# A fused chunked scan and GELU MLP on one core: scan chunks of 128 tokens, and scan halves of 64 tokens laid out by heads

## The chip, the cores and the metric

The kernel runs on one core of a Trainium2 chip. The metric is the device time of one execution in microseconds. The kernel before takes 118.34 us, the median of three runs (118.34 to 118.67).

## The reference

A state-space scan with decay over 4 sequences of 8 heads, 768 tokens, head size 32 and state size 16, and then a two-layer MLP over the 3072 tokens of 8 x 32 = 256 features:

```python
# per batch and head, per chunk of the sequence:
cum = cumsum(log(clip(a)))                     # in the chunk
M = (C @ B.T) * exp(cum_i - cum_j) * (i >= j)  # (chunk, chunk)
y = M @ x + (C @ state) * exp(cum_i)[:, None]
state = exp(sum(log a)) * state + (B * exp(cum_end - cum_j)[:, None]).T @ x
# then, with x = y as (3072, 256):
h = x @ w_in                                   # 256 -> 2048
g = 0.5 * h * (1 + tanh(c * (h + 0.044715 * h**3)))
out = g @ w_out                                # 2048 -> 256
```

The result does not depend on the chunk's length, which the kernel is free to choose.

## The kernel before, in words

**Work.** The 3072 tokens are 24 chunks of 128 tokens (`gc`), taken in 12 pairs `u`; three pairs make one sequence `b`. In each pair the scan leaves y, transposed and in bf16, in `xm`, and the MLP runs over the pair's 256 tokens. The first layer is 8 steps `s1.u.i` of four 128x128 weight blocks against 256 tokens into one of two PSUM tiles `hp` (L710), each followed by `gelu.u.i` on ACT, which writes `gT`. The second layer is, for each of the two chunks, four steps `s2.u.k.q` of four products into `o_ps` (or `yb` for some of the last ones, L728), an eviction `oev` on ACT or DVE and a store. The kernel has 768 such matmuls in all.

**The scan.** B and C come in with the tokens of a sequence spread over partitions, are scaled with the decays (`mul`, `mulb`, `mulc`: B by the decay to the chunk's end, C by its inverse) and turned so that (head, state) lies on 128 partitions: `bh` and, with even and odd heads kept apart by a mask, `ce`. For sequences 0 and 1 TensorE turns them (`tw`, `T1`, `T` with evictions `ew`, `ce1`, `bh1`, `E`); for sequences 2 and 3 they go through DRAM and a transposing DMA (`store_s`, `turn_s`, `load_s`). `N` turns `bh` back to tokens on partitions, `bn`. Then, per pair:
- `G` (L596): the products of B and C, four row strips of 32 partitions (two heads each), one for each of the four banks of `ga` and `gb`; `M` (L606): two DVE products, one for each of the two tiles, with the triangular mask, into `m` in bf16.
- `D` (L629): the chunk's own part of the state, four column strips, into an `hp` tile; `S` (L677): the new state from the old one, on DVE; `SP` (L684): its decayed copy, block-masked by head, in bf16.
- `Y` (L651, L660): for each chunk, eight products of the state with C and eight of x with m, 128 rows deep, in four column strips of 32 outputs, into `yb`; `yev`: the copy to `xm`.
- `castx`: the pair's x from fp32 (128-token rows, loaded by `load_x`) to bf16.

Pairs 0 and 1 get x from one load in another layout: `XX` (L564) unpacks it, `XD` (L574) makes their states, `GE` and `ME` spread the first pair's mask over ACT and POOL.

**The order.** Nothing is scheduled at run time. `ORDERED` (L19) lists every step once, with the engine after a colon where there is a choice (A ACT, D DVE, P POOL, S SyncE); `~n` is n blocks of filler matmuls on zeros (L698). Each engine works through its steps in that order; waits come from the tiles that the steps share. All loads and stores but a few at the start stand in SyncE's queue.

**The start.** The decays of the first four chunks come from `aq`: `clipq`, `Rq`, `tpq`, `peq` on DVE; those of everything else from `a`: `clip` (L329), `R` (L332), `tp2` and `tp6` (L343). Then `mulb`, `mulc`, the turns, `G.0`, `XX.0`, `XD.0`, `M.0`, `Y.0`, `yev.0` lead to the first layer step `s1.0.0`, which also needs the first quarter of w_in, loaded (`load_wi`) and cast to bf16 (`wi.q.k`).

Of the kernel before, what the change touches and what calls it, by code (L numbers as in the profile page):

```python
# [8 lines left out]
FP32 = mybir.dt.float32  # L9
# [6 lines left out]
WFB = 8  # L16
# [8 lines left out]
GE.3 ME.2:P ME.3:P S.0.0 wi.0.1:P M.0.0 wi.1.1:A xn.1:A ~13 XX.1 xn.2:A wi.0.0:A XD.1 ~5 Y.0  # L25
wo.0.0:P wo.0.1:P yev.0.0.2:A G.1 S.0.1 S.1.0 pp mul1.1 S.1.1 M.1.1 M.1.0 pend:A xn.3:A load_wo.2
wi.2.0:P wi.2.1:P s1.0.0 s1.0.1 gelu.0.0 T1.1 ce1.0:D ce1.1:D s1.0.2 gelu.0.1 gelu.0.2 s1.0.3
load_wo.3 SP.3 SP.1 T1.0 s2.0.0.0.o s2.0.1.0.o SP.2 wi.3.1:P bh1:A s1.0.4 gelu.0.3 s1.0.5 G.2 tp6.0
wi.3.0:D tp6.3 gelu.0.4 gelu.0.5 wo.1.1:D Y.1 yev.1.0.2:D wo.1.0:A M.2.0 s1.0.6 s1.0.7 gelu.0.6
s2.0.0.1.o M.2.1 s2.0.1.1.o load_bc.1.0 gelu.0.7 wo.2.0:A s1.1.0 s1.1.1 gelu.1.0 wo.2.1:P  # L30
load_bc.1.1 N1 gelu.1.1 s2.0.0.2.o wo.3.1:A s1.1.2 s1.1.3 tp6.1 tp6.2 mul.1.0 s2.0.1.2.o wo.3.0:P
gelu.1.2 s2.0.0.3.o gelu.1.3 bn1:A oev.0:A recip.1.4 s1.1.4 s1.1.5 load_x.2 s2.0.1.3.o gelu.1.4
T.1.0 mul.1.1 gelu.1.5 castx.2.None:D load_x.3 s1.1.6 oev.1:A s1.1.7 E.1.0:A s2.1.0.0.o T.1.1
gelu.1.6 gelu.1.7 D.2 E.1.1:A N.1 s2.1.0.1.o s2.1.0.2.o s2.1.0.3.o S.2.0 SP.4 bn.1:D F.1
castx.3.None:A Y.2 oev.2:D D.3 G.3 yev.2.0.2:A S.3.0 load_x.4 load_bc.2.0 store.1 s2.1.1.0.o S.3.1
s1.2.0 gelu.2.0 s2.1.1.1.o s1.2.1 s2.1.1.2.o gelu.2.1 s1.2.2 s2.1.1.3.o s1.2.3 M.3.1 M.3.0
castx.4.None:D SP.6 gelu.2.2 Y.3 D.4 gelu.2.3 oev.3:A G.4 S.4.0 S.4.1 s1.2.4 mul.2.0 s2.2.0.0.o
yev.3.0.2:D gelu.2.4 s1.2.5 s1.2.6 gelu.2.5 gelu.2.6 s2.2.0.1.o s1.2.7 SP.8 s2.2.0.2.o gelu.2.7
s1.3.0 gelu.3.0 s2.2.0.3.o s1.3.1 s1.3.2 oev.4:A s2.2.1.0.o s2.2.1.1.o load_bc.2.1 load_x.6 load_x.7
M.4.1 castx.7.None:D mul.2.1 store.2 load_bc.3.1 gelu.3.1 gelu.3.2 s1.3.3 s1.3.4 s2.2.1.2.o  # L40
s2.2.1.3.o store_s.2.0 gelu.3.3 gelu.3.4 s1.3.5 load_x.5 SP.7 M.4.0 SP.9 castx.5.None:P store.3 D.5
Y.4 load_s.2 store_s.2.1 turn_s.2.0 G.5 store.0 turn_s.2.1 load_bc.3.0 oev.5:A gelu.3.5 s1.3.6
s2.3.0.0.o S.5.0 SP.10 castx.6.None:D yev.4.0.2:A gelu.3.6 s1.3.7 s2.3.0.1.o s2.3.0.2.o gelu.3.7
s1.4.0 M.5.1 s1.4.1 M.5.0 s2.3.0.3.o gelu.4.0 D.6 Y.5 store.5 oev.6:D gelu.4.1 D.7 S.6.0 S.6.1 S.7.0
S.7.1 s2.3.1.0.o store.6 load_x.8 s1.4.2 s2.3.1.1.o castx.8.None:P s1.4.3 load_x.11 load_x.9
load_x.10 store.4 yev.5.0.2:A gelu.4.2 s2.3.1.2.o F.2 s1.4.4 gelu.4.3 s2.3.1.3.o gelu.4.4 s1.4.5
mul.3.0 oev.7:A mul.3.1 G.6 s1.4.6 s2.4.0.0.o M.6.0 M.6.1 gelu.4.5 SP.12 s1.4.7 store_s.3.1
store_s.3.0 castx.10.None:P s2.4.0.1.o s2.4.0.2.o gelu.4.6 gelu.4.7 s1.5.0 s1.5.1 gelu.5.0
s2.4.0.3.o gelu.5.1 G.7 oev.8:A D.8 S.8.0 SP.16 M.7.1 Y.6 yev.6.0.2:A s1.5.2 gelu.5.2 s1.5.3
s2.4.1.0.o s2.4.1.1.o gelu.5.3 s1.5.4 turn_s.3.1 turn_s.3.0 s1.5.5 gelu.5.4 gelu.5.5 s2.4.1.2.o  # L50
s2.4.1.3.o s1.5.6 s1.5.7 SP.15 SP.13 oev.9:D gelu.5.6 s2.5.0.0.o s2.5.0.1.o gelu.5.7 s1.6.0 s1.6.1
castx.9.None:P gelu.6.0 gelu.6.1 s2.5.0.2.o s2.5.0.3.o M.7.0 load_s.3 store.7 s1.6.2 oev.10:D s1.6.3
s2.5.1.0.o s2.5.1.1.o G.8 gelu.6.2 castx.11.None:A gelu.6.3 s1.6.4 s1.6.5 s2.5.1.2.o gelu.6.4 M.8.0
s2.5.1.3.o oev.11:D M.8.1 gelu.6.5 s1.6.6 s1.6.7 gelu.6.6 s2.6.0.0.o s2.6.0.1.o D.9 SP.14 S.9.0 F.3
# [34 lines left out]
def kernel(  # L89
# [18 lines left out]
    NCH = batch * CPB  # L108
    HC = CPB // 2
    HS = S // 2  # L110
    T = 2 * Q
    d_ff = moe_w_in.shape[1]
    d_model = moe_w_in.shape[0]
    n_tokens = batch * S
# [224 lines left out]
    def f_Rq():  # L339
        scan(rq_t, acq, Q)  # L340
# [623 lines left out]
```

## Time and profile before

| | |
|---|---|
| median of three runs | 118.34 us |
| the profiled execution | 118.49 us |
| its span, first to last instruction | 116.40 us |
| TensorE clock granted in it | 1.0 |
| TensorE busy with matmuls | 109.9 us, 94% |
| DVE, ACT, POOL busy | 72.0, 73.2, 13.0 us |
| first first-layer matmul (L710) starts | 16.24 us |
| last result leaves PSUM | 113.40 us |

The span runs from the first to the last instruction; what the device time has beside it lies around the program. PE is TensorE's matmuls, PEld its weight loads, and the matmuls' ends are modelled, so for them the starts are what to read. In the slices each digit is the busy share of a fortieth of the span in tenths.

### The profile page before, as it was taken

What the parts mean: (1) busy time and instruction counts of PE and PEld (TensorE: products, weight loads), DVE (VectorE), ACT (ScalarE), POOL (GpSimd) and SP (SyncE); (2) the same over time, 40 slices, a digit from 0 to 9 for tenths busy, and PEclk for the clock granted to TensorE, in tenths of its full rate; (3) what the DMA queues carried; (4) which work ended last, traced back from release to release, by engine and by line L of the source; (5) the groups of instructions that cost most, each with busy time, mean ns of one, the idle gap of its engine ahead of it and who ended that gap; (6) DMA issues with size and microseconds to landing.
All of it is one profiled execution on the core that took longest, in us unless ns stands there. A gap on an engine that the chain in (4) does not pass through costs nothing.

```text
span 116.4 us, 3395 instructions
## 1 busy us (share of the span) xinstructions
PE 109.9 (94%) x1432; PEld 92.6 (80%) x1432; DVE 72.0 (62%) x145; ACT 73.2 (63%) x141; POOL 13.0 (11%) x30
## 2 busy tenths in 40 slices
PE   6949799999999999999999999999999999999990
PEld 2424478899888997898899988778999998999970
DVE  4996889999896994787596149978530152101110
ACT  0425967999756778668666665477477557656701
POOL 6520582400000001002040000000000000000000
PEclk9999999999999999999999999999999999999999
DMA  2999999999978699999946510210001023001212
GB/s 56 273 258 248 308 313 409 336 164 165 247 136 161 185 185 198 86 239 177 177 166 133 160 51 0 93 51 0 6 0 45 0 80 106 0 0 49 92 50 86
DMA packets 43006, 15.97 MB, mean 137 GB/s; under 512 B 36656, under 2 KB 41456, under 8 KB 42992
## 3 DMA queue, kind: packets, MB, share of 16 engines
q1 hardware_dynamic: 42800, 15.67, 55.2%
q8 instruction: 11, 0.18, 0.7%
q10 hardware_dynamic: 192, 0.10, 0.3%
q14 instruction: 3, 0.02, 0.1%
HBM read 11.04 MB, written 3.93 MB: 129 GB/s over the span
## 4 chain that ended last, share of the span: by engine, by line
PE 86%; DVE 6%; ACT 3%; issue 1%; POOL 0%; POOLq 0%; DVEq 0%
PE hp L710 37%; PE o_ps L728 33%; PE ga L596 3%; PE yb L728 3%; PE yb L660 3%; PE yb L651 2%; PE yb L698 1%; PE hp L629 1%; DVE ac L329 1%; ACT ge L611 1%; DVE r_t L332 1%; DVE ce L319 1%; DVE rt L343 1%; DVE unp L262 1%; ACT ce L315 1%
## 5 line engine op out<-in xcount | busy, mean ns | idle before, releaser
L714 ACT ACTIVATE gT<-hp 128x512 bf16<-128x512 f32 x96 | 53.6, 596 | 25.1 <-PE hp L710 24.8
L710 PE MATMUL hp<-xm,w_in_sb 128*128 128x256 bf16 x384 | 51.7, 273 | 0.1
L728 PE MATMUL o_ps<-w_out_sb,gT 128*128 128x256 bf16 x352 | 47.4, 273 | 0.0
L710 PEld LDWEIGHTS <-w_in_sb 128*128 128x128 bf16 x384 | 41.4, 114 | 2.1 <-issue 1.0
L728 PEld LDWEIGHTS <-gT 128*128 128x128 bf16 x384 | 37.1, 98 | 4.2 <-issue 0.4
L319 DVE COPY o_sb<-o_ps 128x256 f32<-128x256 f32 x12 | 5.1, 424 | 24.7 <-PE o_ps L728 22.2
L606 DVE TENSOR_TENSOR m<-ga,tri 128x1024 bf16<-128x1024 f32 x12 | 14.6, 1218 | 3.0 <-PE ga L596 2.0
L606 DVE TENSOR_TENSOR m<-gb,tri 128x1024 bf16<-128x1024 f32 x11 | 13.4, 1216 | 0.0
L698 PE MATMUL yb<-wz 128*128 128x512 bf16 (+3 forms) x32 | 8.6, 410 | 1.0 <-DVE wz L220 1.0
L684 DVE SCALAR_TENSOR_TENSOR sp_new<-s_new,pend,bmask 128x256 bf16<-128x256 f32 x17 | 8.6, 512 | 0.1
L315 ACT ACTIVATE xm<-yb 128x512 bf16<-128x512 f32 x8 | 4.8, 597 | 3.7 <-PE yb L660 2.1
L698 PEld LDWEIGHTS <-wz 128*128 128x128 bf16 x32 | 3.2, 111 | 4.6 <-issue 1.9
L677 DVE SCALAR_TENSOR_TENSOR s_new<-s_new,pend,hp 128x64 f32<-128x64 f32 x13 | 3.6, 278 | 4.9 <-PE hp L629 4.5
L317 POOL CAST x<-x_t 128x512 bf16<-128x512 f32 x4 | 2.6, 669 | 35.2 <-PE hp L710 25.2
L315 ACT ACTIVATE o_sb<-o_ps 128x256 f32<-128x256 f32 x10 | 3.8, 384 | 3.7 <-PE o_ps L728 3.7
L660 PE MATMUL yb<-m,x 128*32 128x128 bf16 x192 | 6.1, 220 | 0.0
L651 PE MATMUL yb<-ce,sp_new 128*32 128x128 bf16 x160 | 5.2, 220 | 0.0
L596 PE MATMUL ga<-ce,bh 32*128 32x256 bf16 x48 | 4.7, 272 | 0.1
L596 PE MATMUL gb<-ce,bh 32*128 32x256 bf16 x48 | 4.7, 273 | 0.0
L728 PE MATMUL yb<-w_out_sb,gT 128*128 128x256 bf16 x32 | 4.3, 273 | 0.0
L660 PEld LDWEIGHTS <-x 128*32 128x32 bf16 x192 | 3.7, 97 | 0.7 <-issue 0.7
L319 DVE CAST xm<-yb 128x512 bf16<-128x512 f32 x4 | 2.7, 683 | 1.6 <-PE yb L660 1.6
(109 smaller groups left out, 76.1 us busy)
## 6 DMA issues: line engine op xcount, KB each, us to landing
out_dram<-o_sb SPq DMA_DIRECT2D x24, 128.0 KB, 2.6
x_t<-in_x_dram SPq DMA_DIRECT2D x20, 128.0 KB, 3.2
wf<-in_moe_w_in_dram SPq DMA_DIRECT2D x4, 512.0 KB, 6.8
wf<-in_moe_w_out_dram SPq DMA_DIRECT2D x4, 512.0 KB, 8.3
bc_t<-in_B_dram SPq DMA_DIRECT2D x3, 384.0 KB, 4.8
bc_t<-in_C_dram SPq DMA_DIRECT2D x3, 384.0 KB, 6.3
scr<-bc SPq DMA_DIRECT2D x4, 192.0 KB, 3.0
x_t<-in_x_dram SPq DMA_DIRECT2D x1, 512.0 KB, 4.5
```

The lines of the kernel that those rows point to most:

```text
L315: nc.scalar.activation(o, i, AF.Copy)
L319: nc.vector.tensor_copy(out=o, in_=i)
L596: nc.tensor.matmul(out=gbank(g)[:, 256 * k:256 * k + 256], lhsT=bh_of(2 * u + k)[gs], rhs=ce_of(2 * u + k)[gs], start=True, stop=True, til ...
L606: nc.vector.tensor_tensor(out=m_of(u)[:, 2 * i:2 * i + 2].rearrange("p g k e t -> p (g k e) t"), in0=gx[i].rearrange("p g (k t) -> p (g k) ...
L651: nc.tensor.matmul(out=y4[32 * j:32 * j + 32, k, w], lhsT=sp[:, 32 * h:32 * h + 32], rhs=ce_of(gc)[:, h % 2], start=first(j), stop=False, ...
L660: nc.tensor.matmul(out=y4[32 * j:32 * j + 32, k, w], lhsT=X16[u][:, k, 32 * h:32 * h + 32], rhs=m[:, h // 2, h % 2, :], start=first(j), st ...
L677: nc.vector.scalar_tensor_tensor(out=s_new, in0=state[("s", gc - 1)], scalar=pend_of(gc), in1=d, op0=ALU.mult, op1=ALU.add)
L684: nc.vector.scalar_tensor_tensor(out=sp_new.rearrange("p (g d) -> p g d", g=4), in0=(XN[0][:, H * D:H * D + 64] if gc == 0 else state[("s" ...
L698: nc.tensor.matmul(out=t[:, 0:m * 128], lhsT=wz, rhs=w3.to_broadcast([128, m, 128]), start=True, stop=True, skip_group_check=True)
L710: nc.tensor.matmul(out=hp[:, j * T:(j + 1) * T], lhsT=w_in_k[:, w, q, k], rhs=xm[:, w, u * T:(u + 1) * T], start=(w == 0), stop=(w == 1))
L714: nc.scalar.activation(gts[u][:, 2 * i:2 * i + 2], hps.pop((u, i)).rearrange("p (j t) -> p j t", j=2), AF.Gelu_apprx_tanh)
L728: nc.tensor.matmul(out=ops[gc], lhsT=gts[u][:, fi, k * Q:(k + 1) * Q], rhs=w_out_sb[:, fi, :], start=(fi == 0 and (u > 0 or k == 0)), stop ...
```

## The change

Pairs 2 to 11 are treated as halves (`n`, 0 to 3 in a pair; `hc` over all) of 64 tokens. Tokens of a half lie on 64 partitions; the lower 64 hold heads 0 to 3 and the upper 64 heads 4 to 7.
- `G`: 16 products of 32 rows by 64 outputs over 64 tokens of the two head parities (128 columns), in `ga`'s two banks only. `MM`: one DVE product of 128x1024 in place of two.
- `D`: 16 products, 64 rows deep, into `yb`. `SS`: one state update per half. `SV`: the decayed, head-masked bf16 copies of up to two states, on POOL or DVE, in place of `SP`.
- `YY`: per half eight products of state and C and eight of x and m, all 64 rows deep with 32 outputs and 64 columns, into the two banks of `gb`; `yev` reads those.
- `castx`: two steps a pair (one for each half of the heads), each with two instructions on 64 partitions. `N`, `N1` and `load_s` lay `bn` out alike: 64x64 products with the identity in place of 128x128 transposes.
- The decay scan restarts every 64 tokens; `endq`, `gpar`, `tri2`, `pm` are new small constants or products. The buffers for fp32 weights go from 8 to 7.
- The whole of `ORDERED` is new. Its start and one later stretch are shown.

```diff
-WFB = 8
+WFB = 7
 ORDERED = """
-c_wz c_ident load_a.1:S c_m4 load_a.0:A c_zero c_unp c_sel load_aq.1:A clip R load_x4 tp2
-load_aq.2:A load_aq.0:A load_aq.3:S load_bc0.0 load_bc0.1 load_wi.1 load_bc1.0 c_warm c_tri x4.0:A
-clipq Rq load_wi.0 c_m8 c_bmask c_par tpq peq mulb:D load_bc1.1 recip0 ~78 ppq ~7 tw.0 ew.0.0:A
-ew.1.0:A recip1 c_cz pendq:D mulc.0:D ~9 tw.1 mulc.1:D ew.0.1:D ew.1.1:A tw.2 load_wo.0 ew.1.2:A
-wi.1.0:A x4.1:P ew.0.2:D load_wi.2 pe load_wi.3 load_wo.1 ~3 XX.0 xn.0:A mul1.0 G.0 XD.0 GE.2 SP.0
...
+c_wz load_aq.1:A load_bc0.0 c_ident c_bmask load_aq.3:A c_zero load_aq.0:S load_aq.2:S c_sel c_unp
+load_bc0.1 load_x4 load_a.0:A load_a.1:S c_m4 c_gpar clipq Rq c_cz c_tri load_wi.0 peq tpq c_tri2
+load_wi.1 load_wo.0 recip0 ~48 ppq mulc.1:D load_wi.2 mulb:P c_m8 load_wi.3 ~18 tw.2 tw.0 c_warm
+ew.0.2:A ew.1.2:A pendq:D mulc.0:D ew.1.0:D ew.0.0:D tw.1 ew.0.1:A load_wo.1 x4.1:A ~9 G.0 clip R
+load_bc1.0 x4.0:P XX.0 load_bc1.1 XD.0 GE.3 S.0.0 SP.0 GE.2 ew.1.1:A xn.1:A xn.0:A ME.3:P ME.2:P ~21
+XX.1 XD.1 M.0.0 wi.0.1:A wi.1.0:D Y.0 S.0.1 xn.2:A pe S.1.0 yev.0.0.2:A wi.0.0:P wo.0.0:P wi.1.1:P
+G.1 tp2 load_x.2 S.1.1 SP.1 M.1.0 load_wo.2 wo.0.1:P pp pend:A s1.0.0 s1.0.1 M.1.1 gelu.0.0 gelu.0.1
...
+E.1.0:A gelu.2.0 mul.1.1 gelu.2.1 T.1.1 E.1.1:A F.1 castx.3.1:D N.1 s1.2.2 s2.1.1.2.o s2.1.1.3.o
+s1.2.3 oev.3:D gelu.2.2 bn.1:A gelu.2.3 s1.2.4 D.3 SS.3.0 SS.3.1 G.3 gelu.2.4 SS.3.2 castx.4.1:D
+SS.3.3 s1.2.5 load_bc.2.1 s2.1.0.0.o MM.3 s2.1.0.1.o s1.2.6 s2.1.0.2.o s2.1.0.3.o mul.2.0 SV.3.0:P
+SV.3.1:P load_x.6 load_x.9 castx.4.0:P D.4 YY.3 castx.5.1:A oev.2:D gelu.2.6 gelu.2.5 G.4 s1.2.7
...
+YX = gx[1][:, :, 0:T].rearrange("p w (n t) -> p w n t", t=L)     # L = 64
+def halves(out, bh, n):                                           # N, N1
+    for k in range(n):
+        for w in range(2):
+            ws = slice(L * w, L * w + L)
+            nc.tensor.matmul(out=out[ws, k], lhsT=bh[ws, L * k:L * k + L], rhs=ident[ws, ws],
+                             start=True, stop=True, tile_position=(L * w, L * w), skip_group_check=True)
 def f_G(u):
+    if u > 1:
+        for k in range(2):
+            for i in range(2):
+                for g in range(4):
+                    gs = slice(32 * g, 32 * g + 32)
+                    w = g // 2
+                    nc.tensor.matmul(out=gx[0][L * w:L * w + L, g % 2, (2 * k + i) * Q:(2 * k + i) * Q + Q],
+                                     lhsT=bh_of(2 * u + k)[gs, L * i:L * i + L],
+                                     rhs=ce_of(2 * u + k)[gs, :, L * i:L * i + L], start=True, stop=True,
+                                     tile_position=(32 * g, L * w), skip_group_check=True)
+        return
...
+def f_MM(u):
+    nc.vector.tensor_tensor(
+        out=m_of(u).rearrange("p g n e t -> p (g n e) t"),
+        in0=gx[0].rearrange("p g (n t) -> p (g n) t", t=L),
+        in1=tri2.rearrange("p (n t) -> p n t", n=1).to_broadcast([128, 16, L]), op=ALU.mult)
 def f_D(u):
-    DT[u] = psh.tile([128, 512], FP32, name="hp")
+    DT[u] = yb[:, 0:T].rearrange("p (n d) -> p n d", d=L)
...
         for g in range(4):
+            ws = slice(L * (g // 2), L * (g // 2) + L)
+            nc.tensor.matmul(out=DT[u][32 * g:32 * g + 32, n],
+                             lhsT=bn_of(gc)[ws, n % 2, 32 * (g % 2):32 * (g % 2) + 32],
+                             rhs=x_of(u)[ws, n, 64 * (g % 2):64 * (g % 2) + 64],
+                             start=True, stop=True, tile_position=(ws.start, 32 * g),
+def f_YY(u):                                                      # mm: start on the first of each (w, j)
+    for n in range(4):
...
+        for part in range(2):
+            if not part and hc % HPB == 0:
+                continue
+            for j in range(4):
+                for w in range(2):
...
+                    if part:
+                        mm(w, j, n, x_of(u)[ws, n, js], MT[u][ws, j // 2, n, j % 2, :], True)
+                    else:
+                        t, c = state[("sp", hc)]
+                        mm(w, j, n, t[ws, c, js], ce[ws, j % 2, ts], False)
+def f_SV(u, q, eng):
...
+    (nc.gpsimd if eng == "POOL" else nc.vector).tensor_tensor(
+        out=t[:, f:2].rearrange("p i (g d) -> p i g d", g=2),
+        in0=sts[:, h0 - 1:h0 - 1 + n].rearrange("p i (o d) -> p i o d", o=1).to_broadcast([128, n, 2, 64]),
+        in1=pm[:, :, b, c + f:c + 2].rearrange("p g (i o) -> p i g o", o=1).to_broadcast([128, n, 2, 64]),
+        op=ALU.mult)
```

More of the change, by code (lines that the diff above doesn't have):

```diff
@@ L25 @@
[L25 to L30, printed above, removed]
@@ L269, in c_par, with c_gpar, c_tri2 @@
                                     op=ALU.add, axis=mybir.AxisListType.X)
+    def c_gpar():
+        bmp = bmask.rearrange("p (w g e d) -> p g w e d", w=2, g=2, e=2)
+        for g in range(2):
+            nc.vector.tensor_reduce(out=gpar[:, g:g + 1], in_=bmp[:, g, :, :, 0], op=ALU.add,
+                                    axis=mybir.AxisListType.XY)
+    def c_tri2():
+        for i in range(2):
+            nc.vector.tensor_copy(out=tri2[L * i:L * i + L], in_=tri[L * i:L * i + L, L * i:L * i + L])
     def c_sel():
@@ L339, in f_Rq @@
     def f_Rq():
-        scan(rq_t, acq, Q)
+        scan(rq_t, acq, endq, Q)
     def turn(o, i, n):
@@ L367, in f_R @@
     def f_R():
-        scan(r_t, ac, HS)
+        scan(r_t, ac, ends, HS)
     def f_tp2():
@@ L679, in f_S, with f_SS @@
                                            op0=ALU.mult, op1=ALU.add)
-        state[("s", gc)] = s_new
+    def f_SS(u, q):
+        hc = 4 * u + q
+        d = DT[u][:, q]
+        if hc % HPB == 0:
+            nc.vector.tensor_copy(out=sts[:, hc % (2 * HPB)], in_=d)
+        else:
+            nc.vector.scalar_tensor_tensor(out=sts[:, hc % (2 * HPB)], in0=sts[:, (hc - 1) % (2 * HPB)], scalar=pend_of(hc), in1=d,
+                                           op0=ALU.mult, op1=ALU.add)
     def f_SP(gc):
-        sp_new = st.tile([128, 256], BF16, name="sp_new")
+        sp_new = spp.tile([128, 256], BF16, name="sp_new")
@@ L689, in f_SP @@
         state[("sp", gc)] = sp_new
+    def f_SV(u, q, eng):
+        b, c = divmod(4 * u + 2 * q, HPB)
+        f = int(c == 0)
+        n = 2 - f
+        t = spp.tile([128, 256], BF16, name="sp_new").rearrange("p (i d) -> p i d", i=2)
+        h0 = (4 * u + 2 * q + f) % (2 * HPB)
+        (nc.gpsimd if eng == "POOL" else nc.vector).tensor_tensor(
[3 more added lines that the diff above has]
+            op=ALU.mult)
+        for i in range(f, 2):
+            state[("sp", 4 * u + 2 * q + i)] = (t, i)
@@ L797 @@
     pp.takes("hp", pd)
+    pm_ = add("D", f_pm, deps=[pd, cgp])
     ce, bh, bn = {}, {}, {}
```

312 lines of the change are left out of this document (178 added, 134 removed).

## The prediction

> **What bounds the kernel now.** I read the page first (busy shares, slices, the chain that ended last), then the chain of waits in order of time, then single stretches of the timeline.
>
> ```profile
> span 116.4 us, 3395 instructions
> PE 109.9 (94%) x1432; PEld 92.6 (80%) x1432; DVE 72.0 (62%) x145; ACT 73.2 (63%) x141; POOL 13.0 (11%) x30
> PE   6949799999999999999999999999999999999990
> DMA  2999999999978699999946510210001023001212
> GB/s 56 273 258 248 308 313 409 336 164 165 247 136 161 185 185 198 86 239 177 177 166 133 160 51 0 93 51 0 6 0 45 0 80 106 0 0 49 92 50 86
> PE 86%; DVE 6%; ACT 3%; issue 1%; POOL 0%; POOLq 0%; DVEq 0%
> ```
>
> TensorE owns 86% of the chain and is full from the sixth slice of 2.91 us on; DVE and ACT have a third of the span free, POOL nine tenths. Before that the transfers are full and the DVE leads the chain.
>
> ```profile
> 6.97 0.24 DVE acq L329
> 15.10 0.23 PE yb L660 x8
> 16.24 0.61 PE hp L710 x4
> 60.48 0.87 PE hp L710 x8
> 61.35 0.87 PE o_ps L728 x8
> 113.40 0.38 ACT o_sb L315
> ```
>
> So there are two parts. **The start** runs until the first first-layer matmul (L710) at 16.24. **The stream** runs from there to 113.40, 97.2 us, when ACT takes the last result. A layer matmul costs 0.87 / 8 = 0.109 us; 768 of them make 83.8. The other 13.3 us are scan products, transposes, changes of the array's shape and the few waits. What follows 113.40 stays as it is: the new order ends in the same copy and store.
>
> **The stream, part by part.** One stretch of TensorE's timeline shows a whole pair:
>
> ```profile
> 30.32 1.36 PE L728 MATMUL o_ps<-w_out_sb,gT 128*128 128x256 bf16 x11
> 31.61 0.29 PE L651 MATMUL yb<-ce,sp_new 128*32 128x128 bf16 x8
> 31.73 0.28 PE L660 MATMUL yb<-m,x 128*32 128x128 bf16 x8
> 31.85 0.28 PE L651 MATMUL yb<-ce,sp_new 128*32 128x128 bf16 x8
> 31.96 0.28 PE L660 MATMUL yb<-m,x 128*32 128x128 bf16 x8
> 32.07 0.23 PE L629 MATMUL hp<-x,bn 128*32 128x64 bf16 x8
> 32.23 0.28 PE L596 MATMUL ga<-ce,bh 32*128 32x256 bf16 x2
> 32.24 0.28 PE L596 MATMUL gb<-ce,bh 32*128 32x256 bf16 x2
> ...
> 32.56 0.61 PE L728 MATMUL o_ps<-w_out_sb,gT 128*128 128x256 bf16 x4
> ```
>
> Outputs (Y): 32 matmuls from 31.61 to 32.07, 0.46 us, 14 ns each, because four column strips of 53 ns run at once. States (D): 8 in 0.16. Gram (G): 8 in 0.33. Eleven layer matmuls would be over at 30.32 + 1.20 = 31.52, yet Y begins at 31.61: a change of shape costs about 0.1 us. Taking it out of D and G as well leaves D 0.06 and G 0.23.
>
> Y becomes YY: 64 matmuls of 64 x 32 strips and 64 columns, eight strips at once. The nearest operation is the state product of pairs 0 and 1, also 64 columns, also eight strips, alternating two banks:
>
> ```profile
> 14.40 0.18 PE L574 MATMUL hp<-x4b,bc0s 32*32 32x64 bf16 x1 [0.48 <-ACT x L315]
> ...
> 14.53 0.19 PE L574 MATMUL o_ps<-x4b,bc0s 32*32 32x64 bf16 x1
> 14.65 0.45 PE L698 MATMUL yb<-wz 128*128 128x512 bf16 x2
> ```
>
> 32 of them start in 0.13 us, 4 ns each, so 64 take 0.26; the upper bound is Y's 14 ns each, 0.90. I take 0.26, the row with the same strips: -0.20 a pair, and **-1.9** over ten, of which three have no state product in their first part. D becomes 16 matmuls of 64 columns on four strips: four rounds instead of two, +0.06, **+0.6**. G becomes 16 of 128 columns on four strips: the same columns streamed, 0. The transposes that make B by token become 64 x 64 products, 32 for 8, with half the columns and two strips at once: 0. Shape changes, counted along the order from the first L710 step to the end: 36 before, 42 after (YY and D share a shape, as Y and D did, but more blocks stand alone), **+0.6**. Sum: **-0.7**.
>
> At one place a rule speaks against this. Before, row strips that run at once write different banks: G's four strips four banks (ga and gb twice), L574's two strips hp and o_ps. In the new G, two row strips share a bank, on different partitions; in the new D, all share yb. No run so far shows that case. The Trainium skill, "TensorEngine Tiling (Array Packing)", section "Gotcha 1: PSUM Pressure", says that different row tiles cannot access the same PSUM bank simultaneously. If strips that share a bank queue, D and G take twice their streams; that is the first rival. I take the value without queueing, because these strips also differ in columns, like Y's, which share a bank.
>
> DVE: one mask product of 1.22 us a pair instead of two, no 512-ns state copies, but four state updates and some SV copies:
>
> ```profile
> L606 DVE TENSOR_TENSOR m<-ga,tri 128x1024 bf16<-128x1024 f32 x12 | 14.6, 1218 | 3.0 <-PE ga L596 2.0 <-PE gb L596 1.0
> L684 DVE SCALAR_TENSOR_TENSOR sp_new<-s_new,pend,bmask 128x256 bf16<-128x256 f32 x17 | 8.6, 512 | 0.1
> L677 DVE SCALAR_TENSOR_TENSOR s_new<-s_new,pend,hp 128x64 f32<-128x64 f32 x13 | 3.6, 278 | 4.9 <-PE hp L629 4.5
> L317 POOL CAST w_in_sb<-wf 128x512 bf16<-128x512 f32 x4 | 2.4, 616 | 1.3 <-DMA wf<-in_moe_w_in_dram 1.3
> ```
>
> About -12.2 - 8.7 + 20 x 0.28 + 5 x 0.5, some 13 us off the DVE. It is worth nothing: the stream hides it. New waits: YY behind SV, of which 15 of 20 sit on POOL. POOL's multiply is not shown; the cast reads 512 elements in 0.62, SV reads 2 x 256, so 0.3 to 1.2, I take 0.6. Behind an SV in POOL's queue stand only input casts; the worst chain, D.3 - three SS - SV - cast - D.4, comes to 0.9 + 0.6 + 0.8 = 2.3 us, beside G.3 and six layer steps of four matmuls, 2.9 us. D now waits for yb instead of hp, which frees hp for the layers. All that: 0, while that cover lasts.
>
> **The start.** Now the DVE does the 64 x 384 clip, scan and turns (3.2 us) ahead of the small ones that feed the first pair:
>
> ```profile
> 3.65 1.06 DVE L274 COPY selp<-sel 128x128 f32<-128x128 f32 x1
> 3.68 0.95 POOL L255 MEMSET cz<- 128x1024 bf16 x1
> 3.79 1.12 DVE L329 TENSOR_SCALAR ac<-a_t 64x384 f32<-64x384 f32 x1
> 4.94 0.95 DVE L332 TENSOR_TENSOR_SCAN r_t<-ac,ends 64x384 f32<-64x384 f32 x1
> 5.92 0.98 DVE L343 STREAM_TRANSPOSE rt<-r_t 32x64 f32<-32x64 f32 x4
> 6.97 0.23 DVE L329 TENSOR_SCALAR acq<-aq_t 128x128 f32<-128x128 f32 x1
> 8.17 0.68 DVE L417 TENSOR_TENSOR bc0s<-bcf,rt 128x512 bf16<-128x512 f32 x1
> 9.21 0.76 DVE L410 TENSOR_TENSOR cz<-bcf,pt 128x256 bf16<-128x256 f32 x2
> ```
>
> The new order puts clipq first and the large steps behind the first pair's evictions, where the DVE otherwise waits for XD. Its own work ahead of clipq would then end near 5.0: the constants up to 3.79, the memset that holds them until 4.63, and four added small ones (0.4). The small loads that clipq needs land then too:
>
> ```profile
> aq_t<-in_a_dram ACTq DMA_DIRECT2D x3, 16.0 KB, 4.4
> ```
>
> They are issued half a microsecond earlier, with B's 256 KB ahead of them instead of x4's 512 KB, so 4.4 us is their upper bound and 5.0 a fair landing. From clipq to the first mulc lie 2.24 us now, 0.6 of them mulb. mulb moves to POOL, 0.6 (one cast) to 1.2 us (two operands of 512; I take this), from 6.4 to 7.6. The memset row shows that the copy and the clip, short otherwise, both end only after POOL's memset at 4.63. So I let mulc wait for mulb as well and put the second mulc's end at 8.4; not waiting would be worth 0.7. The Trainium skill, "SBUF — State Buffer", section "Who interferes with whom", calls the ports that the two engines share an exclusive lock, for the copies' modes and for a two-input DVE product against a reading POOL. The trace agrees for the copy and the clip (1.06 and 1.12 us); no run so far shows the product.
>
> From the last mulc's end, 9.97, to the first L710 lie 6.3 us now. The new chain from 8.4 is two evictions on the DVE (0.9), G.0, ACT's cast of x4 until 10.0, XX and XD until 10.5, then SP 0.5, M 1.2 and their hand-overs until 12.5, Y 0.5, its eviction 0.7 and the one small product pp ahead of the layers: 5.7 us. The first L710 comes at **14.1**, **-2.1**. Bounds: 12.9 (no blocking and a short mulb) and 15.7 (the small loads as late as now).
>
> Part of it is paid back. The weight casts of now start when their loads land (DMA row: saturated until slice 11):
>
> ```profile
> 16.49 1.18 POOL L317 CAST w_in_sb<-wf 128x512 bf16<-128x512 f32 x2 [0.20 <-DMA wf<-in_moe_w_in_dram]
> 18.81 0.62 POOL L317 CAST w_in_sb<-wf 128x512 bf16<-128x512 f32 x1 [1.14 <-DMA wf<-in_moe_w_in_dram]
> 21.37 0.62 POOL L317 CAST w_out_sb<-wf 128x512 bf16<-128x512 f32 x1 [1.94 <-DMA wf<-in_moe_w_out_dram]
> ```
>
> Moving the two small B and C loads (0.26 MB) behind wo.1 brings wi.3 about 1 us forward at 0.3 MB/us, to 17.7; two POOL casts, which queue behind wi.2's, end at 18.9. The stream would want them at 18.4: **+0.5**. wo.2 comes 0.6 later (x.2 and the small loads ahead of it), 2 us before need; wo.3, on seven buffers, waits for the first casts at 12.5, and the B and C loads of sequence 1 behind it on SP are then still early. ACT, with 9 us of work beside 9.5 of TensorE where pair 1's second half meets wo.3's casts and E.1, may add **+0.3**.
>
> **Sum.** -0.7 - 2.1 + 0.8 = -2.0 against the profiled execution's 118.49 (span 116.40 and 2.09 around it): **116.5**. The median shown is 118.34, 0.1% under it.
>
> **Rivals.**
> 1. *Row strips queue at a shared bank* (slower). D +0.12 and G +0.23 a pair and B's products, twice as long, +0.4: +3.9, so 120.4. It turns the sign once more than 2.0 us are lost, half of this. For it: every row-strip product now in the kernel writes banks of its own. Against: Y's column strips share one.
> 2. *The loads set the start anyway.* If weights land no earlier than now, wi.3's casts end at 19.9, 1.0 behind the forecast, and wo.1's at 21.3, another 0.5: the payback is 2.3 instead of 0.8, and 118.0 is left. For it: DMA full in slices 2 to 11. Against: casts of now are done 1 us and more ahead of use.
> 3. *The start goes better*: no blocking, 12.9, and no payback: -0.7 - 3.3: 114.5.
> 4. *TensorE cannot be fed 64 small products at 4 ns.* The 32 at 14.40 had waited 0.48 us behind ACT, so they may have been queued. At 8 ns YY takes 0.51, +2.5: 119.0; at Y's 14 ns, 122.9.
> 5. *The order adds waits* in mid-stream (POOL slower than 1.2, a load late): +3, 119.5.
>
> **Chances.** Forecast 50%, rival 1 13%, 2 13%, 3 13%, 4 5%, 5 6%. Differences within 0.3% (0.36 us) are what a measurement of this kernel cannot tell from none. Faster: 46 of the forecast's 50, rival 3, and 5 of rival 2, 64%; same: 3 + 6, 9%; slower: 27%. The range leaves out rival 4 and the far ends of 3 and 5, and takes in rival 1: 114.2 to 120.6.
>
> **What would show it.** The first L710 at 14.1 (12.9 to 15.7) and clipq near 5.0. YY's 64 starts in 0.26 us; D's 16 in 0.12 and G's in 0.23, twice that under rival 1. TensorE's digits 9 from slice 6 on, no wait over 0.3 us after 25 us. DVE near 60 us busy. It is wrong if TensorE sits idle for SV, MM or casts past pair 3, or if the first L710 stays near 16.

## The result, and the profile after

The changed kernel takes 121.75 us, the median of four runs (120.11 to 123.43), beside 118.44 us for the kernel before on the same chip (118.34 to 118.67, four runs). The ratio is 1.0158, with an interval of 1.0132 to 1.0185: 1.6% longer, some 120.3 us by the ratio, where 116.5 us and faster had been forecast. Some executions of a kernel are up to 4 us longer than its others; the ratios leave those out, and of the profiles read below three are of such executions, those of 123.43 us (changed kernel), 120.08 us (experiment 3) and 122.88 us (`start_weights`).

The page of an execution of 119.92 us (experiment 1 below), 1.43 above the profiled execution of before. TensorE, slices, transfers, chain:

```profile
span 118.2 us, 4471 instructions
PE 112.3 (95%) x1931; PEld 95.5 (81%) x1931; DVE 65.1 (55%) x165; ACT 75.4 (64%) x146; POOL 25.7 (22%) x55
PE   6979999999999999999999999999999999999990
DMA  3999987997999767999994940021001201021102
PE 78%; DVE 7%; DMA 7%; SPq 3%; issue 2%; ACT 0%; DVEq 0%
```

TensorE is now full from the fourth slice on, and stays so to the end. The kernel is slower although its bounding engine starts earlier and hardly idles: the time is in what TensorE does. Its timeline where the layers begin (L820 is the first layer's matmul here, L710 before):

```profile
14.16 0.39 PE L416 MATMUL hp<-pe,selp 64*128 64x48 f32 x2 [0.29 <-DVE pe L410]
14.48 1.06 PE L820 MATMUL hp<-xm,w_in_sb 128*128 128x256 bf16 x8
```

The stream starts 1.76 us earlier, at 14.48 for 16.24, and all of that and as much again is lost behind it. The table adds up the time from each matmul's start to the next one's, by kind, from the first layer matmul to the last; a change of shape and a wait fall to the matmul ahead of them. The third column is an experiment, the changed kernel behind the old start, told below.

| us | before | changed | changed, old start |
|---|---|---|---|
| first layer matmul | 16.24 | 14.48 | 16.91 |
| 768 layer matmuls | 85.47 | 85.90 | 85.81 |
| outputs (Y; YY and the Y of pair 1) | 5.49 | 6.53 | 6.06 |
| states (D) | 0.95 | 2.26 | 2.27 |
| B times C (G) | 3.29 | 3.63 | 3.68 |
| turns (T, N) | 1.65 | 1.83 | 1.82 |
| filler on zeros | 0 | 0.21 | 0.21 |
| stream | 96.85 | 100.38 | 99.86 |

The outputs were to fall by 1.9 us; they rose, by 1.04, of which 0.4 is a wait in the Y of pair 1, and by 0.57 behind the old start, where that wait is missing. One step YY in TensorE's timeline (start, busy time, then the tile, the shape of the strip and the count):

```profile
26.50 0.82 PE L820 MATMUL hp<-xm,w_in_sb 128*128 128x256 bf16 x6
27.25 0.22 PE L698 MATMUL gb<-ce,sp_new 64*32 64x64 bf16 x8
27.29 0.21 PE L698 MATMUL gb<-m,x 64*32 64x64 bf16 x8
27.32 0.21 PE L698 MATMUL gb<-ce,sp_new 64*32 64x64 bf16 x8
27.35 0.21 PE L698 MATMUL gb<-m,x 64*32 64x64 bf16 x8
27.48 0.26 PE L698 MATMUL gb<-ce,sp_new 64*32 64x64 bf16 x8
27.54 0.26 PE L698 MATMUL gb<-m,x 64*32 64x64 bf16 x8
27.61 0.26 PE L698 MATMUL gb<-ce,sp_new 64*32 64x64 bf16 x8
27.68 0.26 PE L698 MATMUL gb<-m,x 64*32 64x64 bf16 x8
27.86 0.72 PE L838 MATMUL o_ps<-w_out_sb,gT 128*128 128x256 bf16 x5
```

Read the starts. The first four groups of eight come 30 to 40 ns apart, 4 ns a product, as forecast. Then there is a pause (27.35 to 27.48), and the last four come 60 to 70 ns apart, over 8 ns a product. From the first to the 64th start it is 0.49 us, and 0.61 to the next layer matmul. Nine of the ten YY steps of this execution break at the 33rd product. Three of the nine have 56 products (the first half of a sequence has no state product), and there the 33rd is another product, in the middle of the third half:

```profile
65.32 0.21 PE L698 MATMUL gb<-ce,sp_new 64*32 64x64 bf16 x8
65.45 0.26 PE L698 MATMUL gb<-m,x 64*32 64x64 bf16 x8
```

In the tenth step 16 products of D, of the same strips, are mixed in, and the row breaks behind the 32nd of both kinds together, which is YY's 16th.

### The profile page after: what moved, and what is told of

Read it like the earlier page. It is cut to its first block, busy times and chain, and to the rows that moved or that the text cites. A ratio compares the mean times of both kernels' runs of the same rounds, so it can differ in the third digit from the quotient of the medians.

```text
span 121.7 us, 4471 instructions
## 1 busy us (share of the span) xinstructions
PE 113.3 (93%) x1931; PEld 96.0 (79%) x1931; DVE 65.5 (54%) x165; ACT 75.5 (62%) x146; POOL 25.9 (21%) x55
## 4 chain that ended last, share of the span: by engine, by line
PE 64%; SPq 15%; DMA 10%; DVE 5%; issue 2%; POOL 1%; ACT 0%; POOLq 0%
PE hp L820 27%; PE o_ps L838 25%; SPq L161 5%; DMA bc_t<-in_B_dram 5%; DMA x_t<-in_x_dram 5%; PE gb L698 4%; SPq L181 3%; PE yb L838 3%; PE ga L638 3%; SPq L196 2%; SPq L200 1%; PE yb L688 1%; DVE x L342 1%; DVE m L658 1%; SPq L168 1%
## 5 line engine op out<-in xcount | busy, mean ns | idle before, releaser
L820 PE MATMUL hp<-xm,w_in_sb 128*128 128x256 bf16 x384 | 52.9, 274 | 0.2 <-POOL w_in_sb L340 0.2
L820 PEld LDWEIGHTS <-w_in_sb 128*128 128x128 bf16 x384 | 41.0, 114 | 2.4 <-POOL w_in_sb L340 0.4
L793 POOL TENSOR_TENSOR sp_new<-sts,pm 128x256 bf16<-128x256 f32 (+1 forms) x15 | 8.8, 595 | 55.2 <-DVE sts L775 48.1
L775 DVE SCALAR_TENSOR_TENSOR sts<-sts,pend,yb 128x64 f32<-128x64 f32 x33 | 9.2, 278 | 3.8 <-PE yb L688 3.2
L808 PE MATMUL yb<-wz 128*128 128x512 bf16 (+2 forms) x26 | 8.3, 475 | 1.1 <-DVE warm L231 1.1
L342 DVE CAST x<-x_t 64x256 bf16<-64x256 f32 x22 | 7.3, 334 | 1.5 <-DMA x_t<-in_x_dram 1.2
L340 POOL CAST x<-x_t 64x256 bf16<-64x256 f32 x12 | 5.2, 430 | 8.5 <-DMA x_t<-in_x_dram 8.0
L698 PE MATMUL gb<-m,x 64*32 64x64 bf16 x320 | 6.5, 194 | 0.1
L698 PE MATMUL gb<-ce,sp_new 64*32 64x64 bf16 x296 | 6.0, 195 | 0.0
L638 PE MATMUL ga<-ce,bh 32*64 32x128 bf16 x160 | 4.4, 220 | 1.7 <-DVE ce L544 1.7
L698 PEld LDWEIGHTS <-sp_new 64*32 64x32 bf16 x296 | 4.5, 89 | 1.2 <-issue 0.8
L698 PEld LDWEIGHTS <-x 64*32 64x32 bf16 x320 | 4.9, 89 | 0.6 <-issue 0.6
```

Of the source, the lines that this page charges most:

```text
L342: nc.vector.tensor_copy(out=o, in_=i)
L638: nc.tensor.matmul(out=gx[0][L * w:L * w + L, g % 2, (2 * k + i) * Q:(2 * k + i) * Q + Q], lhsT=bh_of(2 * u + k)[gs, L * i:L * i + L], rhs ...
L698: nc.tensor.matmul(out=YX[32 * j:32 * j + 32, w, n], lhsT=lhsT, rhs=rhs, start=(w, j) not in fresh, stop=stop, tile_position=(L * w, 32 * ...
L775: nc.vector.scalar_tensor_tensor(out=sts[:, hc % (2 * HPB)], in0=sts[:, (hc - 1) % (2 * HPB)], scalar=pend_of(hc), in1=d, op0=ALU.mult, op ...
L793: (nc.gpsimd if eng == "POOL" else nc.vector).tensor_tensor(out=t[:, f:2].rearrange("p i (g d) -> p i g d", g=2), in0=sts[:, h0 - 1:h0 - 1 ...
L808: nc.tensor.matmul(out=t[:, 0:m * 128], lhsT=wz, rhs=w3.to_broadcast([128, m, 128]), start=True, stop=True, skip_group_check=True)
```

## The experiments

In the rows of waits, the engine, tile and line that waited stand left of the arrow and what released them right of it; then come the us in all, the number of waits and the longest. Two theories stood against each other. **Issue**: TensorE has some 32 small products ready when it comes to them, and what lies behind is fed at over 8 ns each. **Transfers**: the loss is waits for loads that the new order makes late. For the second spoke the waits of the execution profiled first, that of 123.43 us:

```profile
PE ga L638 <- DVE ce L544: 1.7, 1, 1.7
PE yb L688 <- DVE x L342: 0.6, 1, 0.6
```

G.7 waits for sequence 2's turned C, and D.2 for pair 2's x; before has neither.

**1. The changed kernel again, with no edit.**

> The changed kernel as it is, for a profile of an undisturbed execution. Two theories stand for the loss. Issue: TensorE holds some 32 small products ready; what comes beyond them starts 8.3 ns apart instead of 4, so that an output step (YY) takes 0.5 us instead of 0.26 and the scan products and shape changes cost about 2.5 us more than before, in every execution. Transfers: the loss is waits for loads (x of pair 2, the turned C of sequence 2), 4 us in the execution profiled so far, and the products are as forecast. Issue expects 120.1 to 120.7 us with YY at 0.5 us and waits of 1 us or less in all; transfers expects waits that differ from execution to execution and still add to 2 us or more here.

120.94 us (119.92 to 123.33), ratio 1.0120 (1.0096 to 1.0144). The waits of the execution of 119.92:

```profile
PE yb L808 <- DVE warm L231: 1.1, 1, 1.1
PE hp L455 <- POOL m L259: 0.5, 1, 0.5
PE hp L416 <- DVE pe L410: 0.3, 1, 0.3
PE hp L808 <- ACT gT L824: 0.2, 1, 0.2
PE yb L736 <- DVE sp_new L780: 0.2, 1, 0.2
```

The first three lie ahead of the layers. Neither D.2 nor G.7 waits, and the kernel still takes 1.2% longer than before. Waits for loads make 2.3 us of the execution of 123.43; they do not explain this one.

**2. The changed kernel behind the old start.**

```diff
-c_wz load_aq.1:A load_bc0.0 c_ident c_bmask load_aq.3:A c_zero load_aq.0:S load_aq.2:S
+c_wz c_ident load_a.1:S c_m4 load_a.0:A c_zero c_unp c_sel load_aq.1:A clip R load_x4 tp2
...
 s1.0.0 s1.0.1
```

> The changed kernel with the old start and the new order behind it, first matmul near 16.2. Issue: the stream's loss of 2 to 3 us stands alone, 121 to 122 us. Transfers: with the loads in the old order the stream is as forecast, 118 to 119 us.

122.47 us (121.86 to 122.57), ratio 1.0317 (1.0288 to 1.0347). Its list of waits, whole:

```profile
PE yb L806 <- DVE wz L226: 1.1, 1, 1.1
PE hp L377 <- DVE peq L372: 1.0, 1, 1.0
PE hp L607 <- ACT x L336: 0.5, 1, 0.5
PE hp L806 <- ACT gT L822: 0.2, 1, 0.2
PE hp L597 <- ACT ce L336: 0.2, 1, 0.2
```

Only the 0.2 of L806, the filler, lies in the stream. So the last column of the table is a stream without transfer waits, and it is 3.0 us longer than that of before: outputs +0.57, D +1.32, G +0.39, layers +0.34, filler 0.21, turns 0.17. The new start is worth about 2 us to the changed kernel (121.86 against 119.92).

**3. Half the products in YY.** The kernel leaves out the products of state and C in pairs 2 to 11.

```diff
-                if not part and hc % HPB == 0:
+                if not part:
                     continue
```

> The changed kernel without the products of state and C in pairs 2 to 11 (the output then lacks what comes from earlier halves), so that an output step has 32 products instead of 64. Issue: 32 are held ready and start in 0.13 us, 0.38 less a pair, 3 to 3.8 us less in all: 116.8 to 117.8. Transfers: 32 products at 4 ns are 0.13 less a pair, 1.3 at most, and the waits for the turned C swallow part: 119.2 to 120.

118.88 us (117.37 to 120.67, ten runs), ratio 0.9985 (0.9951 to 1.0018). Its YY:

```profile
28.75 0.31 PE L698 MATMUL gb<-m,x 64*32 64x64 bf16 x32
28.99 0.72 PE L838 MATMUL o_ps<-w_out_sb,gT 128*128 128x256 bf16 x5
```

32 products and the change of shape take 0.24 us instead of 0.61, and L698 2.50 us in all instead of 5.54. Half the products cost two fifths of the time, and the whole disadvantage is gone with them. The time meets neither expectation: by the ratios it is 1.6 us below that of the changed kernel, where L698 saves 3.0. In the one profiled execution, of 120.08 us, G.7 waits 1.5 us and D.2 0.5 for loads; where the rest goes in the shorter ones no profile shows. So YY's products carry the loss; that does not yet say whether the second 32 are slow because they are the second 32.

**4. YY in two steps of 32**, a few layer steps apart; everything is computed.

```diff
-    def f_YY(u):
+    def f_YY(u, half):
-        for n in range(4):
+        for n in (2 * half, 2 * half + 1):
...
-YY.2 s2.0.0.3.o s2.0.1.3.o gelu.1.6
+YY.2.0 s2.0.0.3.o s2.0.1.3.o YY.2.1 gelu.1.6
```

> The changed kernel with each YY step cut in two steps of 32 products (two heads each), the second two layer steps behind the first (one layer step for pair 6); everything else as in the changed kernel. Issue (some 32 small products are held ready, what lies behind them starts 8.3 ns apart): now each half finds its 32 products ready, 0.13 us each with 0.1 us per additional change of shape, so L698 falls from 0.5 us a pair to 0.26 in starts, and the time stays or falls by about 0.5 us (10 x (0.25 - 0.2)), 119.4 to 120.1. If 8.3 ns is instead a property of the second half of the products themselves (their banks, columns or operands) and not of a stock that ran out, the second halves still start 8.3 ns apart, the changes of shape come on top, and the time is about 2 us higher, 122. Transfers: no change in the waits, 120 as before.

123.49 us (122.88 to 124.96), ratio 1.0390 (1.0355 to 1.0426). By the time alone that would be the second alternative. The timeline says otherwise (L699 is YY here, L839 the second layer):

```profile
26.92 0.22 PE L699 MATMUL gb<-ce,sp_new 64*32 64x64 bf16 x8
26.96 0.21 PE L699 MATMUL gb<-m,x 64*32 64x64 bf16 x8
26.98 0.21 PE L699 MATMUL gb<-ce,sp_new 64*32 64x64 bf16 x8
27.01 0.21 PE L699 MATMUL gb<-m,x 64*32 64x64 bf16 x8
27.16 1.05 PE L839 MATMUL o_ps<-w_out_sb,gT 128*128 128x256 bf16 x8
28.14 0.22 PE L699 MATMUL gb<-ce,sp_new 64*32 64x64 bf16 x8
28.18 0.21 PE L699 MATMUL gb<-m,x 64*32 64x64 bf16 x8
28.20 0.21 PE L699 MATMUL gb<-ce,sp_new 64*32 64x64 bf16 x8
28.23 0.21 PE L699 MATMUL gb<-m,x 64*32 64x64 bf16 x8
```

Both halves start within 0.12 us, and the second half does so in all ten pairs. The very products that came at 8.3 ns come at 4 ns when layer matmuls stand ahead of them; the second of the two theories of the pace falls. And the added time:

```profile
PE hp L821 <- ACT xm L337: 1.7, 2, 0.9
PE hp L821 <- DVE xm L341: 0.4, 1, 0.4
PE o_ps L839 <- DVE o_sb L341: 0.3, 1, 0.3
```

2.4 us of new waits: the second halves stand so late that the layers wait for the copy of y. Without them the kernel would be near the unsplit one. In the rows the split saves 0.25 us a pair of pace (0.12 twice for 0.49) and adds two changes of shape at about 0.1.

**5. Two attempts on the transfer waits.** The DMAs of sequence 2's turned C and B ahead of other loads, and pair 2's x ahead of the two small loads of pair 2's B and C (`load_bc1`; the expectations, here and below, call them sequence 1's):

```diff
-store.1 load_x.7 load_x.8 ... load_s.2 store_s.2.1 ... turn_s.2.1 ... turn_s.2.0
+store_s.2.1 load_x.7 turn_s.2.0 load_x.8 turn_s.2.1 load_s.2 ... store.1
```
```diff
-load_bc1.0 x4.0:P XX.0 load_bc1.1 ... G.1 tp2 load_x.2
+load_x.2 load_bc1.0 x4.0:P XX.0 load_bc1.1 ... G.1 tp2
```

> The changed kernel with the DMAs of sequence 2's turned C and B (the second store, the two turns) issued ahead of the x loads of pairs 7 and 8 and of store.0 on SP, where they stood behind them. Transfers: the wait of G.7 for the turned C of sequence 2 (1.9 us in the profiled run of the changed kernel) is gone in every execution, so the slowest executions come about 1.9 us down, the lower ones, which had no such wait, stay near 120.0. Issue: the same for the lower ones; L698 stays at 0.5 us a pair, and the kernel stays about 1.2% slower than the kernel before.

> The changed kernel with pair 2's x load issued ahead of the two loads of sequence 1's B and C, where it stands behind them. Transfers: D.2 never waits for x (1.3 us in the profiled run of the changed kernel), so the slowest executions lose that, and the lower ones stay near 120.0 unless B and C of sequence 1 (T1) now come late, which would cost up to 1 us. Issue: no change of the lower executions, 119.9 to 120.3; L698 stays at 0.5 us a pair.

The first took 127.53 us (126.51 to 128.03), ratio 1.0737 (1.0692 to 1.0783): a miss. Its largest wait in the profiled execution (127.85 us):

```profile
PE yb L686 <- DMA bn<-scr: 3.9, 2, 3.4
```

D.6 now waits for the untransposed B of the same sequence, which was issued behind the turns; a new wait took the place of the old. Behind its 3.4 us the granted clock is 0.58 of full speed from 55.5 to 58 us and 0.78 from 58 to 61, which by an estimate from these figures costs up to another 1.7 us. The second took 121.36 us (120.64 to 124.86), ratio 1.0233 (1.0203 to 1.0263): 1% more than the changed kernel, not less, though its profiled execution (120.64) shows no wait in the stream above 0.3. One execution of five took 124.86 us; it has no profile, so whether D.2 waited in it is not shown. What makes the loads late in some executions and not in others is left open.

**6. The new start with the old pairs.** Eight kernels, all the kernel before with another order, which begins as the changed one does. In `start_alone` the new order goes up to `s1.0.1`, in `start_alone2` up to `s1.1.3`, in `start_long` up to `s1.1.7`, and the old order follows with what is left. `new_order_old_pairs` has the new order throughout, each old step at its counterpart's place. `start_best` is `start_alone2` without the filler and with two steps moved. In `start_weights` the loads of wo.2 and wo.3 are also issued ahead of `load_bc1`'s two, and T1 and G.2 come later; in `start_weights2` `load_bc1`'s two stand between wo.2 and wo.3; in `start_weights3` mul.1.0 is also moved ahead of M.2.1, and T.1, D.3 and G.3 later. Two cuts show pair 3 in `new_order_old_pairs` beside the changed kernel (-), and `start_best` beside `start_alone2` (-):

```diff
-castx.3.0:P ... castx.3.1:D ... D.3 SS.3.0 SS.3.1 G.3 ... MM.3 ... SV.3.0:P SV.3.1:P ... YY.3
+castx.3.None:D ... D.3 S.3.0 G.3 S.3.1 ... M.3.0 M.3.1 ... SP.6 ... Y.3
```
```diff
-wo.0.0:P wi.1.1:P G.1 tp2 load_x.2 ... s1.0.2+4
+wi.1.1:P wo.0.0:P G.1 tp2 ... s1.0.2 ... s1.1.5 load_x.2
```

> The kernel before with the new order's start alone (everything up to the first first-layer matmul, its loads too), then the old order. Issue: the start is worth what the first matmul shows, it begins near 14.6 instead of 16.24, so 116.9 to 117.4 us. Transfers: the loads give it back, one of the casts of the weights or x of pair 2 comes late and 118 to 119 us remain.

> The kernel before with the changed kernel's order up to layer step s1.1.3, so that the loads and the products of sequence 1's B and C stand where the changed kernel has them, and the old order, old pairs 2 to 11, from there on. The start was worth -1.8 us at the first layer matmul and the stream cost +3.5, so this kernel should keep the first without the second. Issue: first L710 near 14.5, the stream within 1 us of before's 96.9 (the filler of four products +0.2, up to +0.8 given back in waits for weights or in sequence 1's steps), 117.0 to 117.9, faster than before. Transfers: the same start, but the loads of pairs 2 to 4 land later as they do in the changed kernel, and the stream gives back 2 us or more, so 118.5 or above.

> As the run with the new start and the old pairs, with three edits: no filler products on s1.0.2, the cast of wi.1.1 ahead of that of wo.0.0 on POOL (its wait was 0.4 us in the changed kernel), and pair 2's x load left at its old place behind the B and C loads of sequence 1. Issue: 0.2 to 0.6 us below that run, 116.6 to 117.5, a version below both kernels. Transfers: pair 2's x lands later still, and its D waits: 0.5 us or more above that run.

> The kernel before, its pairs 2 to 11 unchanged (Y of 128-row products, two mask products, state copies on the DVE), but everything in the changed kernel's order: the new start, the loads, weight casts, B and C of the sequences, layer steps and stores where the changed kernel has them, each step of an old pair at the place of its new counterpart. Issue (the halves themselves cost the stream 3 us, and the order's only cost is small): Y 5.5, D 0.95, G 3.3 as before, first layer matmul near 14.5, so about 117 us, below both kernels, if the longer mask products (2.4 for 1.2 us a pair) find cover at those places; up to 1 us more if not. Transfers (the order's loads and waits are what costs): the waits stay with the order, and it stays at 119.5 to 120.5 like the changed kernel.

> As the run before it in this call, but only up to the layers of pair 2 (all weight casts and sequence 1's products B and C in the new order, which the shorter version of this experiment cut in two), the old order from there on. Issue: the lead of 1.7 us is kept past the weights, less 0.2 for the filler, so 117.0 to 118.0. Transfers: the loads behind the start are late and the lead is lost, 118.7 or above.

> The kernel with the new start, old pairs and old order from pair 2 on (no filler), with the loads of wo.2 and wo.3 issued ahead of the two loads of sequence 1's first B and C, their casts at once behind them, and the products that need that B and C (mul1, T1, N1 and G.2) four layer steps later. In the earlier run wo.3 landed at 25.35 (22.66 in the kernel before) and the layers waited 0.7 us for its cast and some 1 us for B and C. If eight outstanding DMAs ahead of the weights are what ate the lead (loads theory): wo.3 lands near 22, no wait for w_out, first layer matmul near 14.7 and 117.2 to 118.2, below both kernels. If not (the old pairs themselves need the time between pair 1 and pair 2): 119 as the earlier run.

> As the run before it in this call, with the two loads of B and C between wo.2 and wo.3 instead of behind both. Loads theory: wo.3 lands near 23, B and C about 1 us earlier than in that run, 117.2 to 118.5. Otherwise 119 as the earlier run.

> As the last run, with sequence 1's first product (mul.1.0) between pair 2's two mask products on the DVE instead of behind them, and its turns T.1, N.1 and pair 3's D.3 and G.3 two to four layer steps later. In the last run the weights no longer waited, and what was left was one wait of 1.9 us of T.1 for that product. Loads theory: with it gone the stream is within 1 us of before's 96.9 behind a first layer matmul near 14.7, 117.2 to 118.2, below both kernels. Otherwise a new wait takes its place and it stays at 119 or above.

| kernel | median, us | ratio | interval | largest new wait of TensorE, us in all |
|---|---|---|---|---|
| start_alone | 124.54 | 1.0485 | 1.0451 to 1.0519 | T1 for a mask product queued on the DVE, among others behind two products that wait 1.2 for loads, 5.5 |
| start_alone2 | 119.80 | 1.0058 | 1.0026 to 1.0091 | second layer for w_out's cast, 1.2 |
| start_best | 119.21 | 1.0057 | 1.0032 to 1.0081 | the same, 0.7 |
| start_long | 120.89 | 1.0190 | 1.0150 to 1.0230 | Y for its state copies, 1.2 in 2 |
| new_order_old_pairs | 129.43 | 1.0901 | 1.0852 to 1.0951 | first layer for hp, 5.8 in 11 |
| start_weights | 121.59 | 1.0236 | 1.0201 to 1.0271 | T.1 for its product on the DVE, 2.1 |
| start_weights2 | 120.57 | 1.0180 | 1.0137 to 1.0223 | the same, 1.9 |
| start_weights3 | 121.51 | 1.0242 | 1.0205 to 1.0279 | D.2 for hp, 1.5 |

All take longer than before, by 0.6% to 9%, although in all of them the layers begin at 14.6 to 15.2. Expected were some 117 to 118 in most, so here Issue's expectation failed each time; its account of YY is not touched by that, for there is no YY in these kernels. Two of the rows, from the waits of the whole new order with the old pairs and of the last kernel:

```profile
PE hp L707 <- ACT gT L711: 5.8, 11, 0.7
```
```profile
PE hp L626 <- ACT gT L711: 1.5, 1, 1.5
```

In the old pairs D lies in an hp tile, so the layers have one tile left until S has read it. The new order was written for D in yb, and with D in hp it stalls eleven times. The other kernels trade one wait for the next: when the weights came early (start_weights2: no wait for a cast left), T.1 was late; when T.1 was moved, D.2 was. The waits do not account for everything: the stream of `start_best` is 99.12 us, 2.3 over before's, and its waits add to 1.4. Part of the loss in two of these kernels is the clock. Behind the wait of 5.5 us in `start_alone` the granted clock is 0.50 of full speed from 21.5 to 24 us and 0.57 from 24 to 27; behind that of 2.1 in `start_weights` it is 0.69 from 30.3 to 34 and 0.82 from 34 to 37. By an estimate from these figures that costs up to 2.5 and 1.7 us. In `start_weights2`, with a wait of 1.9, the clock stays at 1.0. So the start is not a part of the change that could be had alone in these orders, and none of them beats both kernels. Whether one that does exists is open.

## Why the prediction was wrong

**The step that failed is YY's 0.26 us.** The prediction took "32 of them start in 0.13 us, 4 ns each, so 64 take 0.26". The row's pace was right and the 64 products do begin at 4 ns; but the row held 32 products and no further ones of their kind, so it showed a rate for 32. (Its strips were also 32 rows by 32 columns, not YY's 64 by 32; the pace of the first 32 is the same.) The 33rd comes 0.1 us after the 32nd and the rest at 8.3 ns: 0.49 to the last start, 0.51 to the next layer matmul when 0.1 is taken off for the change of shape. Over ten pairs 0.25 us each are 2.5 us, more than the whole gain of 2.0 that was forecast. It is rival 4 at 8 ns, which was given 5% because its one doubt, that the 32 "may have been queued", had no second row to weigh it with. Experiments 3 and 4 show that the count decides and not the products: 32 alone take 0.12, and so do either 32 of the same 64. The steps of 56 and the one with D mixed in say the same.

The Trainium skill, "TensorE: Matmul & The Clock Gate", section "Architectural detail: the array is 16× 32×32, not 1× 128×128", gives TensorE's queue as 64 instructions; by an estimate from it these are 32 weight loads with their 32 matmuls. The trace agrees: the pace breaks behind the 32nd. That it is this queue which runs empty is the likely cause, but no run shows the queue itself. What sets the 8.3 ns thereafter no run here shows.

**D, G and the changes of shape** were to cost 1.2 us (0.6 and 0 and 0.6). Without transfer waits, the third column of the table, everything but the outputs costs 2.4: D 1.32, G 0.39, layers 0.34, filler 0.21, turns 0.17. The products themselves are as forecast:

```profile
34.06 0.30 PE L688 MATMUL yb<-x,bn 64*32 64x64 bf16 x16
34.29 0.42 PE L638 MATMUL ga<-ce,bh 32*64 32x128 bf16 x16
34.64 0.63 PE L820 MATMUL hp<-xm,w_in_sb 128*128 128x256 bf16 x4
```

D takes 0.23 to G's start and G 0.35 to the layer's; less 0.1 for the change of shape they are 0.13 and 0.25, for 0.12 and 0.23. So **rival 1 falls**: row strips that share a bank did not queue, which would have been 0.24 and 0.46. The Trainium skill's rule in "TensorEngine Tiling (Array Packing)", section "Gotcha 1: PSUM Pressure", that different row tiles cannot use one PSUM bank at once, cost nothing in these two steps. The changes of shape are 36 and 42 in the traces, as counted; with them a pair's D takes 0.23 where it took 0.10 (2.27 and 0.95 over ten). What the forecast left out are the four blocks of filler that the order adds, the small turns, and short pauses, such as 0.24 us in which pair 3's outputs stand behind D.4 until their mask product ends on the DVE; not all of them were traced.

**The start** was nearly right: 14.48 for 14.1, inside its bounds. The DVE's first steps:

```profile
5.32 0.23 DVE L352 TENSOR_SCALAR acq<-aq_t 128x128 f32<-128x128 f32 x1 [1.39 <-DMA aq_t<-in_a_dram]
7.30 0.78 DVE L439 TENSOR_TENSOR cz<-bcf,pt 128x256 bf16<-128x256 f32 x1
8.07 0.41 DVE L439 TENSOR_TENSOR cz<-bcf,pt 128x256 bf16<-128x256 f32 x1
```

clipq came at 5.32 (5.0 forecast), and it was the loads that held it; the second mulc ended at 8.48 (8.4). POOL's mulb beside it:

```profile
6.72 1.07 POOL L446 TENSOR_TENSOR bc0s<-bcf,rt 128x512 bf16<-128x512 f32 x1 [2.60 <-DVE rt L365]
```

1.07 us for the 1.2 taken. The first mulc began 0.5 us before mulb's end and took 0.78; the second, alone, took 0.41. So the two were in each other's way. The Trainium skill's "SBUF — State Buffer", section "Who interferes with whom", would have the DVE's product wait until POOL's ends at 7.79. That agrees in direction, but leaves it 0.29 us for what takes 0.41 alone. The other 0.3 us went into the chain from there to the layers.

**The payback** was 0.8 by forecast. Old start against new, the stream is 99.86 and 100.38: 0.5. The last casts of w_in end at 18.48 (18.9 forecast):

```profile
16.00 2.48 POOL L340 CAST w_in_sb<-wf 128x512 bf16<-128x512 f32 x4
```

Start and payback together, -1.3 by forecast, came out at -1.24. **Rival 2** (loads set the start anyway) is not what happened to the changed kernel; with the old pairs, experiment 6, late loads and casts did take back part of the start.

**The DVE** is 65.1 us busy instead of some 60 (the casts on 64 partitions were left out), and no wait in the stream shows that it is worth anything. SV on POOL was a good guess:

```profile
L793 POOL TENSOR_TENSOR sp_new<-sts,pm 128x256 bf16<-128x256 f32 (+1 forms) x15 | 8.7, 585 | 54.9 <-DVE sts L775 48.2
```

585 ns for 0.6, and no YY waited for it. **Rival 5** (waits in mid-stream, +3) describes the execution of 123.43 us, with 2.3 us of waits in the two rows quoted above, and not that of 119.92.

Sum for the execution of 119.92: start -1.76, stream +3.53, around the span -0.37 (1.72 for 2.09), together +1.4. Of the 3.4 us between that and the forecast of 116.5, 2.5 are YY's pace and 1.2 what D, G and all between the products cost beyond their forecast; the 0.37 around the span, which was not forecast, hides part of it. That 119.92 lies inside the range given is luck: the top of the range was set by rival 1, which did not happen. Two sums of the prediction are slightly off and change nothing: 768 times 0.109 is 83.7, and -0.20 a pair with -0.11 for the three that lack a state product is -1.7 and not -1.9.

## What to carry to other kernels

A rate read from a burst is a rate for a burst of that length: before a short run of small products is scaled up, look for a longer one in the trace, or put the break at the length that was seen. Many small products pay per block, about 0.1 us for each change of shape, so a change that multiplies their number or splits their blocks must win that back first. An order written for one use of the buffers is not a part that can be tried alone: moved to a kernel that holds another tile for longer, it stalls there, and a long stall can cost clock on top.

## What the runs showed of the hardware

- Small matmuls on eight strips of 64 rows and 32 columns start about 4 ns apart for 32 of them, then pause 0.1 us, then start 8.3 ns apart.
- Eight layer matmuls, 0.87 us, were enough for the next 32 products to start at 4 ns again (experiment 4).
- Behind waits of TensorE of 5.5, 3.4 and 2.1 us the granted clock fell to 0.50, 0.58 and 0.69 of full speed for some us; behind waits of 1.9 (`start_weights2`) and 1.7 us (execution of 123.43) it stayed at 1.0.
- A DMA issue can hold SyncE for long: in the changed kernel the load of pair 2's C took 5.54 us to issue, and the two behind it 3.89. Why is not settled. The kernel before has such an issue too, 4.60 us for a C load.

```profile
9.13 5.54 SPq L161 DMA_DIRECT2D bcf<-in_C_dram  x1
14.71 3.89 SPq L181 DMA_DIRECT2D x_t<-in_x_dram  x2
```
